# Strip attention on one core: 255 instead of 251 score tiles taken off ScalarE, in a new order, with GpSimd's constant add written another way

## The chip, the core and the metric

The kernel runs on one core of one Trainium2 chip. The metric is device time in microseconds (us), the median over several executions of the same program. Engines are called by the profile's names: PE is TensorE (matmuls), PEld its weight loads, DVE is VectorE, ACT is ScalarE, POOL is GpSimd, and SP is SyncE, which here only issues DMAs.

## The reference

An image of 224 x 224 pixels with 96 channels is projected to q, k and v. The first 48 channels attend inside horizontal strips 8 rows high, the last 48 inside vertical strips 8 columns wide; each strip has 1792 tokens, there are 28 strips of each kind. Both results are projected by `wo`.

```python
qkv = jnp.einsum('bhwc,cd->bhwd', x, wqkv)
q, k, v = qkv[..., :C], qkv[..., C:2*C], qkv[..., 2*C:]
scale = C2 ** (-0.5)                       # C = 96, C2 = 48, sw = 8, H = W = 224
qh, kh, vh = (t[..., :C2].reshape(B * nh, sw * W, C2) for t in (q, k, v))
ah = _softmax(jnp.einsum('bqc,bkc->bqk', qh, kh) * scale, axis=-1)
oh = jnp.einsum('bqk,bkc->bqc', ah, vh).reshape(B, H, W, C2)
# qv, kv, vv, av, ov: the same over vertical strips, channels C2 to C
o = pad(oh) + pad(ov)                      # side by side in the channels
return jnp.einsum('bhwc,cd->bhwd', o, wo)
```

The inputs are bf16: x of shape (1, 224, 224, 96), wqkv (96, 288), wo (96, 96).

## The kernel before

**Tiling.** Two strips are worked on together as one strip pair P, 28 in all: 0 to 13 horizontal, 14 to 27 vertical. Queries come in four chunks of 512, 512, 512 and 256 columns, keys in 14 blocks of 128. A score tile is one key block against one query chunk for both strips, 128 x 1024 values (for the last chunk two key blocks share one tile). PE makes the scores, something takes their exponential into a slot of `PT` (28 slots), and PE multiplies the slot by V and adds it up in one PSUM bank (the PV step).

**Who takes the exponential.** Mostly ACT, one ACTIVATE of 128 x 1024 for each tile (line 939, `emit_qk`). ACT's scores go to two fixed sets of two PSUM banks, in turn. The tiles listed in `KINDS`, one row for each P and one string for each chunk, are taken off ACT and get a polynomial in the bits of the result, of which there are two kinds in use:

- a **P tile**: DVE makes a scaled score q into `qb` (line 1082, two half tiles), POOL squares it (line 1110), adds a constant (line 1111) and squares again (line 1106); PE computes the scores a second time, and DVE adds them to the result as an integer (line 1087, two half tiles).
- an **R tile**: DVE makes q (line 1082) and a product with the scores (line 1084), two half tiles each, POOL squares (line 1106), PE computes the scores a second time, and DVE finishes (line 1087).

So a P tile is three POOL and four DVE instructions, an R tile one POOL and six DVE instructions. Some pairs of half tiles go through DVE as one instruction of 128 x 1024. Scores for DVE go to a ring of four PSUM banks, shared with PV sums and with the preparation of later strip pairs.

**Other work.** DVE also evicts the projections K, Q, V (lines 594, 603, 641), the PV sums (`OT`, line 958) and the output rows (`og`, line 709). A DMA transpose on SP turns `OT`; DVE takes reciprocals (line 1030) and POOL multiplies by them (line 1045, the norms, 54 in all). At the end POOL issues a few of the output DMAs.

**The order.** While the program is built, a planner walks the string list `ORDER`, one string for each P, a letter for each PE step: q is an ACT tile's scores, 1 and 3 the first and 2 and 4 the second scores of a P or R tile, v a PV step, k, g and f preparation and output steps. PE's instruction order is these strings, word for word. The planner keeps a clock for each engine from constants at the head of the file, and with it decides the order of DVE's and POOL's instructions (`dve_step`, `pool_step`), which slots and banks are used, and where SP's transfers stand. At run time each engine goes through its fixed list, and waits on semaphores of the engines (one count for each instruction) for what it reads or overwrites. POOL's instruction also waits for an earlier POOL instruction whose result it reads. When PE goes from scores (mode `A`, with f) to PV and preparation (mode `B`) or back, the planner adds a price, `SW_AB` or `SW_BA`.

The constants of the planner that matter here are its prices for POOL, in us: `D_SQ` for a product, `D_AF` for the constant add, `SEMP` for the time until a POOL result is seen; a norm's price is worked out in `dve_step` when its reciprocal is queued.

Of the kernel before, what the change touches and what calls it, by code (L numbers as in the profile page):

```python
# [30 lines left out]
    ["PR", "P", "PPRR", ""],
    ["RRPP", "RP", "PRRP", ""],
    ["RP", "RP", "PPPRR", ""],
    ["PRR", "P", "PPPRR", ""],
    ["PPRR", "P", "PRPRP", ""],
    ["PRR", "P", "PPRP", ""],
    ["PR", "RRP", "PPPRRP", ""],
    ["RR", "PP", "PPRRP", ""],
    ["PRP", "PPPR", "RP", ""],
    ["RP", "P", "RPPPRR", ""],  # L40
    ["RPR", "P", "PPPRPR", ""],
    ["RRP", "P", "PPRRP", ""],
    ["PR", "RPPPR", "PR", ""],
    ["PP", "RRPPR", "P", ""],
    ["PPPR", "RPP", "RRPP", ""],
    ["PR", "PPPRP", "P", ""],
    ["PPR", "R", "PPRP", ""],
    ["PPPRR", "PP", "R", ""],
    ["PPPP", "RR", "PRPP", ""],
    ["PPR", "R", "PPPP", ""],  # L50
    ["PPP", "RRRPR", "PP", ""],
    ["PPR", "PP", "RRPP", ""],
    ["PR", "PPP", "RRPP", ""],
    ["PP", "PP", "PRR", ""],
    ["PPP", "RRPR", "RPP", ""],
# [24 lines left out]
D_V2 = 0.6  # L80
# [4 lines left out]
    "vvq2vqv1qkvvqvvq2qvvqkvkq1qkvqvkvq1vqvkqkqkvvq2qvkvq1qkvqvvq1qvvvqkvqv4qvvq2qvvq1q1qvvkqvvvqv2qvq2qv2qvq2vqv1qvvq",
    "2vqvvvq2vqv3qvvqkkq1vqkvq1qkvvqkvq1vqvvvqv2qvvqkvvqkqk1qkqvvvqv1qvvqvvqv2qvvq1qvkq1qvvkq1qvvvkqvvq2qvvq2qvv1qvq2vqv2qvvvqv2qvq",
    "1vvq4qvvkqkkq1qvvkqvvvq1qvvvqkvq2vqvkvq1qvvq1qkvqvvqv2qvvq1qvkq2qvkqkvkq3qvvqvvqvvvq2qkvvq1vvq2qvv2qvvq2vqv1qvvqv1qvvq",
    "2vqv1qvvqk2qvkqkvq1qkvvqkvqv1qvkvqvvqv2qvvqv2qvvq1qvkq2qvkq1qkvqvvq1vvqvvqkvqvvqv2qvvq2vqv1qvvq2vqkvq2vqv3qvvvqk2qvvq1vvq",
    "2qvv1qvq2vqkvqkkvq1qkvqvkvqv1qvkqvvqv3qvvqv2qvvq1qvkq2qkvq1qkvqvvq1vvqvvqv2qvvqvvqvkq2vqv1qvkqv2qvvq2vvq2qkvvq2vqvvq1vq",
    "v2qvvqv1qkvvqvvqv1qvkqkvq1qkvvqkq2vqvkvq1qvvqk2qvvq1qvkq1qkvqvvq1vqvvvqv2qvvqkvqvvq2vqv1qkvqv2qvvq2vvq2qvv3qvvqv2qkvvq",  # L90
    "1qvv2qvvqkkqk1qvqkvvqvkvq2qvkvq1qvkq1qvkq1qkvqvvqv2qvkqvvq1qkvqvvq1vqvvqvv2qvvqvvqv2qkvvq1qvv1qvq2vvq2qvv2qvvq1vqvvq2vqv2q",
    "vvq1vqv1qvkvqvvq2qvvqkkvq1qkvqvkvq1vqvkqkqkvvq4qkvvq1qkqvvvq1vqvvvqv2qvvq1qvvq2qvvvq2vqv2qvvq2vqv1qvvq2vqkvkqvvq1vvq",
    "1qvv4qvvqk2qvkqkvq1qkvqvkvq1vqvvqvvq2vqvkvqv1qvvq1qvkq2qvkq1qkvqvvvq2qvvkqkvqv1qkvqvvvq2vqv2qvvq2vqv1qvvq2vvq1qvvq2vvqv2q",
    "vvq1vqv2qkvqkvq1qkvvqvkqv1qvvqvvvq1vqvkvqkqk2qvvq2qkvq1qkvvqvq1vvqkvq2qkvq2qvvq3vqvvq1vkqvvqv1qvvqv2qvvq2vvq2qvvq2vqvv2q",
    "vvq1vqvkq1vqkvq1qkvqvvkvq1qvvqvkvq2vqvkqkqkvvq1qkvvqvvq1vqvkqkvq1qkvqvv2qvvq2qvqvvq2vvq1qvv2qvvq2vqv2qvvq1vqvvq2vvq1qvv1q",
    "vq2vqv1qvvkqvvvq1vqvkqkvq1qkvqvvq2qvvkqv2qkqkkqkqk1qvvkqvvqv1qvvqvvqv1qvvqkvvq2qvkvqv2qvvq1vvq2qvv2qvq2vvq1qvv2qvvqv2q",
    "vvq1vqvkq2vqkvq1qkvqvvkvq1qvvvqvvq2vqvkvqkqk1qvvq1qvkqkkq1qkvqvvq1vqvvqvv2qvqvvq2vqvv2qvvq2qvv1qvq2vvq1qvv2qvqkvvq1vvq2q",
    "vv2qvqv1qkvqvvvq1vqvkqkvq1qkvvqkvq2vqvkqkvvq1qvvgqkqkvgqgkqkvqv2qvvq2vqv1qvvq2vqv1qvvvqvq1vqvvqvv1qvqv2qkq2qvvq3vqvvq2vvq",
    "2qvv2qvvqkkqkq1vqkvvqvvkq1qvgvqkgqkqkvq2vqv1qvkqkvq1vqgvvqvgq2vqkvqkgvq2vqv2qvvq1vqgvq2vqv1qvvqvvq1vqvvqvv1qvvqgvqgvq1vqvvq2vq",
    "v2qvvq2vqv1qvgvqvvq1vqvvqvv2qvqkvqkvkqkvvq1qvvkq3qkvvq2vqv2qvvq4vqgvq2vqvkq1vqv1qvvqgvqvvqkgqkkqgqgvq1vvq4qkvvq2qkvvq",  # L100
    "2qv1qvvvqv1qvvq2vqvkqk2qvvqgvkq1qkvvqkvq1vqvkqkvqgvq4vqgvq1vqvkqk2qvvqkvq1vqkvqkvgq2vqv2qvvq2vqvgq1vqv1qvvgqvvqv1qvvqvvgqv4qvvq",
    "v1qvvqv2qvvq1vq4qvvkqkq1kqvvkqvvkq2qvvqkvvq3vqvgq4vqgvq2vqv2qvvqkvq1vqv1qgvqvkq2vqv2qkvqkvq1vqkvq1vqvvvqv1qvvqvvkqv4qvvqv4qvvq",
    "v1qvvq2vqv1qvvqk1qvvqkvvqvkqkvqggvqkgqk2qvvvq2vqv3qvvqg2qvvqv1qvgqvkq2vqv1qgvqvkq4vqvgq1vqkkqkvqv1qvvkqvgqvvq1vqvgvqvvq1vqvvq2vq",
    "vvvq2vqv2qvvqkkqk1qvqkvvqvvq2vqvvq1vkqv1qvkqv2qvvqk4qvvqvgq2vqv1qgvqkvq1vqkgqv4qvkqv1qkvqvvqvvq1vqvkvqvvq4vqvvq2vvqv1qvvq",
    "v2qvvq1vqv2qvkqkkqvvkqggqkvqg1qvkqkgqkqkkqkvvq2vqv1qvvq1vqgvq2vqv2qvvqv1qkvvq2vqv2qgvqv1qgvqv2qgvqv1qvvqvvgqv1qvvqvvqv1qvvvqvvq",
    "vvqv2qvvq1vqvkq2kqvvq1qvvkqvvqkvvq2qvv1qkvq3vqvvq2vqv2qgvqgvgqkvqkq2vqkvq1vqkkqv2qgvqv2qvkqv1qvvqkvgq1qgvvqvvq2vqvvq2vvq",
    "1qvvvqv1qvvq2vqv4qvvqk1qvkqvvvq1qvvvqvvq2vqvvqkkvqv1qvvqkgq1vqkvq2vqvkq2vqv1qgvqvkq2vqv4qvvqk1qvvqvkqvvkqgvq1qkvvq2vqv2qvvq",
    "1vqv2qvvqgvq1vqv4qvvqk1qkvqvvqv1qvvqvvq2vqvgqkvqgvkqgvvqk1qvvq1vqkvq2vqkvq2vqv1qgvqvkq2vqv1qvvqg2qvvqkkqgvgqgvqkkvqv2qvvq2vq",
    "v1qvvq1vqv2qvvvq2qvv1qvvqkkq1qvkvqvvkqv1qvqvvvq4qvvvqkgqgkqvvq2vqkvq1vqv1qgvqkvq2vqv2qvkqvkq4vqkvq1vqv1qvvgqvvqv1qvvqvvqgvqv2qvvq",
    "kvvq1vqv2qvvq2vqv1qvgvqvvq1vqvvqvvq1vqvkqkvkqvvq2vqkvqvkgq1vqkvq2vqv1qgvqkvq2vqv2qvgqvkqvgqg1qvvqkkqgvkq2qvkvqv1qvvq2vqv2q",  # L110
    "vvq1vqvvvq2vqv1qvvq1vqvvqv1qvvqvvvq2vqvgqgvqgvq1vqvvq2vqv2qvvq2vqv1qvvfqv1qvfqv2qvfqvvfqvvfqv2qvvfqgvqgvq2vqv2qvvgqfvq4fqqvvvvvfffvvvfff",
# [106 lines left out]
def bass_standalone__window_attn_cswin__vision_kernel(  # L218
# [28 lines left out]
    with es:  # L247
# [844 lines left out]
        def mids_w(tl):  # L1092
            g, gk = gb[tl["gb"]], [("g", tl["gb"], 0), ("g", tl["gb"], 1), "pser"]
            l = g.bitcast(U16).rearrange("p (n t) -> p n t", t=2)[:, :, 0]
            y, yk = PT[tl["slot"]][:], pt_keys(tl["slot"])
# [2 lines left out]
            return [("pool", D_AF, lambda e: e.tensor_scalar(z, l, WK ** 0.5 * 2.0 ** -16, -WK ** 0.5 * t0, ALU.mult, ALU.add), gk, yk),
                    ("pool", D_SQ, lambda e: e.tensor_tensor(z, z, z, ALU.mult), yk + ["pser"], yk),
                    ("pool", D_AW, lambda e: e.tensor_tensor(g[:], g[:], z, ALU.add), gk + yk, gk[:2]),  # L1100
                    ("pool", D_AG, lambda e: e.tensor_scalar(y.bitcast(U16), g[:], c, 1.0, ALU.add, ALU.mult), gk, yk),
                    ("pool", D_AG, lambda e: e.tensor_scalar(PT[tl["slot2"]][:].bitcast(U16), g[:], c + 64.0, 1.0, ALU.add, ALU.mult), gk, pt_keys(tl["slot2"]))]

        def mids(tl):
            y, yk = PT[tl["slot"]][:].bitcast(FP16), pt_keys(tl["slot"])
            square = ("pool", D_SQ, lambda e: e.tensor_tensor(y, y, y, ALU.mult), yk + ["pser"], yk)  # L1106
# [3 lines left out]
            return [("pool", D_SQ, lambda e: e.tensor_tensor(y, q, q, ALU.mult), qk, yk),  # L1110
                    ("pool", D_AF, lambda e: e.tensor_scalar(y, y, -(QS * (RB + RA) / 2) ** 2, 1.0, ALU.add, ALU.mult), yk + ["pser"], yk),  # L1111
                    square]
# [521 lines left out]
```

## Time and profile before

| what | value |
|---|---|
| median of 3 runs | 1047.13 us (1046.86 to 1047.49) |
| the profiled execution's own time | 1047.03 us |
| its span, first to last instruction | 1045.2 us |
| granted TensorE clock, mean | 0.999 |
| busy: PE, DVE, ACT, POOL | 1024.8, 1027.6, 1034.9, 1001.9 us |
| ACT tiles, P tiles, R tiles | 1121, 155, 96 |

A row of a group reads: line, engine, operation, out<-in by the program's names, shape, xcount, then busy us and the mean ns of one, then the engine's idle time just before these instructions and what ended it. A row of the timeline reads: start in us, duration in us, engine, line, operation; equal neighbours are merged (x2), and a wait stands in brackets. Busy time is the union of the instructions' durations; where durations overlap, the step from start to start is shorter than a duration. Line numbers are those of the kernel before.

### The profile page before, as it was taken

The page shows a single profiled execution, that of the slowest core. Times are in us where ns is not written, and L with a number is a line of the kernel's source. Part 1 is how long each engine was busy: PE and PEld are TensorE (multiplying, and loading weights), DVE is VectorE, ACT ScalarE, POOL GpSimd, SP SyncE. Part 2 cuts the span into 40 slices and gives each one's busy share as a digit, 9 for nine tenths or more (in the row PEclk, how much of TensorE's full clock was granted, in tenths as well). Part 3 has the DMA queues.
Part 4 walks back from the last instruction along what each step waited for, and adds up shares of the span by engine and source line. Part 5 has one row for each costly group of instructions (what it writes and reads, how often), then busy time and mean ns, then how long its engine had stood idle before and what let it go on. Part 6 is the DMA issues. An engine that isn't in the chain of part 4 may idle for free.

```text
span 1045.2 us, 33013 instructions
## 1 busy us (share of the span) xinstructions
PE 1024.8 (98%) x13456; PEld 388.6 (37%) x13456; DVE 1027.6 (98%) x1905; ACT 1034.9 (99%) x1131; POOL 1001.9 (96%) x662
## 2 busy tenths in 40 slices
...
GB/s 175 166 181 126 131 24 140 119 52 125 147 93 71 130 108 81 28 59 59 15 91 114 60 93 103 101 58 94 95 49 104 105 100 44 104 102 49 71 79 60
DMA packets 414199, 96.84 MB, mean 93 GB/s; under 512 B 404928, under 2 KB 411296, under 8 KB 414048
## 3 DMA queue, kind: packets, MB, share of 16 engines
...
q0 software_dynamic: 128, 0.20, 0.1%
...
## 4 chain that ended last, share of the span: by engine, by line
PE 59%; DVE 24%; ACT 8%; issue 4%; POOL 4%; DMA 1%; POOLq 0%; ACTq 0%; SPq 0%; DVEq 0%
PE ps L788 23%; PE ps L761 20%; PE ps L774 10%; ACT PT L939 8%; DVE qb L1082 7%; DVE PT L1087 7%; DVE PT L1084 3%; PE ps L589 3%; DVE KT_sb L594 2%; PE ps L703 2%; POOL PT L1106 2%; PE ps L634 2%; DVE OT_sb L958 1%; DVE QT_sb L603 1%; POOL PT L1110 1%
## 5 line engine op out<-in xcount | busy, mean ns | idle before, releaser
L939 ACT ACTIVATE PT<-ps 128x1024 bf16<-128x1024 f32 x1121 | 1030.3, 1091 | 0.6 <-PE ps L761 0.2
L1106 POOL TENSOR_TENSOR PT<-PT 128x1024 f16<-128x1024 f16 x251 | 470.4, 1893 | 8.6 <-DVE PT L1084 1.0
L788 PE MATMUL ps<-PT,V_sb 128*49 128x512 bf16 (+1 forms) x3136 | 470.1, 362 | 0.3 <-DVE PT L1087 0.2
L761 PE MATMUL ps<-QT_sb,KT_sb 49*64 49x512 bf16 (+1 forms) x5292 | 456.4, 361 | 2.6 <-ACT PT L939 1.5
L1082 DVE TENSOR_SCALAR qb<-ps 128x512 f16<-128x512 int16 x490 | 329.8, 697 | 3.2 <-PE ps L761 0.3
L1087 DVE SCALAR_TENSOR_TENSOR PT<-ps,PT 128x512 uint16<-128x512 f32 (+1 forms) x479 | 323.0, 709 | 5.2 <-PE ps L774 0.9
L1110 POOL TENSOR_TENSOR PT<-qb 128x1024 f16<-128x1024 f16 x155 | 291.9, 1892 | 9.8 <-DVE qb L1082 6.5
L761 PEld LDWEIGHTS ps<-QT_sb,KT_sb 49*64 49x64 bf16 x5292 | 136.9, 104 | 264.0 <-ACT PT L939 240.3
L774 PE MATMUL ps<-QT_sb,KT_sb 54*64 54x512 bf16 (+1 forms) x2008 | 202.6, 394 | 11.7 <-DVE PT L1087 2.7
L788 PEld LDWEIGHTS ps<-PT,V_sb 128*49 128x49 bf16 x3136 | 133.2, 103 | 202.6 <-issue 169.8
L1111 POOL TENSOR_SCALAR PT<-PT 128x1024 f16<-128x1024 f16 x155 | 161.8, 1044 | 13.0
L1084 DVE SCALAR_TENSOR_TENSOR PT<-ps,qb 128x512 f16<-128x512 int16 (+1 forms) x190 | 128.0, 688 | 0.6
L774 PEld LDWEIGHTS ps<-QT_sb,KT_sb 54*64 54x64 bf16 (+1 forms) x2008 | 56.8, 103 | 101.0 <-DVE PT L1087 34.2
L958 DVE CAST OT_sb<-ps 113x512 bf16<-113x512 f32 x111 | 68.5, 617 | 0.1
L603 DVE CAST QT_sb<-ps 128x512 bf16<-128x512 f32 (+1 forms) x111 | 67.5, 615 | 0.1
L594 DVE TENSOR_SCALAR_CACHE_REDUCE KT_sb<-ps 128x512 bf16<-128x512 f32 x108 | 64.4, 616 | 0.0
L709 DVE CAST og<-ps 128x480 bf16<-128x480 f32 x84 | 50.8, 616 | 0.2
L641 DVE CAST V_sb<-ps 128x480 bf16<-128x480 f32 (+1 forms) x84 | 50.8, 617 | 0.1
L589 PE MATMUL ps<-xT_sb,wq_sb 97*64 97x512 bf16 x224 | 41.5, 368 | 0.0
L589 PE MATMUL ps<-xT_sb,w_sb 97*64 97x512 bf16 x224 | 39.8, 369 | 0.0
L634 PEld LDWEIGHTS ps<-w_sb,xT_sb 96*64 96x64 bf16 x1568 | 33.6, 112 | 16.3 <-issue 7.5
L634 PE MATMUL ps<-w_sb,xT_sb 96*64 96x48 bf16 x1568 | 39.3, 190 | 0.0
...
## 6 DMA issues: line engine op xcount, KB each, us to landing
...
```

What stands on the lines that cost most here:

```text
L589: ins = e.matmul(bk[64 * w:64 * w + 64, 0:qs], lhsT=lw, rhs=xT_sb[b][0:C + 1, w, q0:q0 + qs], start=True, stop=True)
L634: ins = e.matmul(bk[64 * h:64 * h + 64, j * C2:(j + 1) * C2], lhsT=xT_sb[b][0:C, w, t0:t0 + 64], rhs=w_sb[0:C, wblk(P, "v"), 0:C2], start= ...
L761: ins = e.matmul(bank(SETS[s] + w)[64 * kh:64 * kh + 64, i * t["qs"]:(i + 1) * t["qs"]], lhsT=KT_sb[b][64 * w:64 * w + CA, kt * 128 + 64 * ...
L774: ins = e.matmul(bank(bp[w])[64 * kh:64 * kh + 64, 0:512], lhsT=KT_sb[b][64 * w:64 * w + nr, kt * 128 + 64 * kh:kt * 128 + 64 * kh + 64], ...
L788: ins = e.matmul(bank(pb)[64 * w:64 * w + CA, 0:t["qs"]], lhsT=V2_sb[b][:, w, kt - NKT + NV2, :] if second else V_sb[b][:, w, kt, :], rhs= ...
L939: S.commit("act", 0.0, D_ACT, None, lambda e, s=s, slot=slot: e.activation(PT[slot][:], ps[:, 512 * SETS[s]:512 * SETS[s] + 1024], ACTF.Ex ...
L1082: fn, reads, writes = lambda e: e.tensor_scalar(q, l, m, a, ALU.mult, ALU.add), bk, qk
L1084: fn, reads, writes = lambda e: e.scalar_tensor_tensor(y.bitcast(FP16), l, -RA * 2.0 ** 16, q, ALU.add, ALU.mult), bk + qk, ptk
L1087: fn, reads, writes = lambda e: e.scalar_tensor_tensor(y.bitcast(U16), f, 128.0, y.bitcast(FP16), ALU.mult, ALU.add), bk + ptk, ptk
L1106: square = ("pool", D_SQ, lambda e: e.tensor_tensor(y, y, y, ALU.mult), yk + ["pser"], yk)
L1110: return [("pool", D_SQ, lambda e: e.tensor_tensor(y, q, q, ALU.mult), qk, yk), ("pool", D_AF, lambda e: e.tensor_scalar(y, y, -(QS * (RB ...
L1111: ("pool", D_AF, lambda e: e.tensor_scalar(y, y, -(QS * (RB + RA) / 2) ** 2, 1.0, ALU.add, ALU.mult), yk + ["pser"], yk),
```

## The change

Four things are edited; all else stays.

1. `KINDS`: 157 P and 98 R tiles instead of 155 and 96, 1117 ACT tiles instead of 1121, most rows different.
2. `ORDER`: all 28 strings are new.
3. The planner's prices for POOL: a product 1.852 instead of 1.9, the constant add 1.01 instead of 1.03, 0.125 more (`D_TS`) for a constant add that follows a product or a norm, 0.13 instead of 0.10 until a result is seen, a norm's fixed part 0.14 instead of 0.18. They steer the order of DVE's and POOL's instructions.
4. POOL's constant adds compute x times 1 plus c instead of x plus c times 1. Of the lines that have this, only line 1111 is used here: `KINDS` has no W and no Q tiles.

```diff
 KINDS = [
-    ["PR", "P", "PPP", ""],
-    ["RPR", "PP", "RRPRR", ""],
...
-    ["PP", "P", "PPRRPPP", ""],
+    ["PR", "P", "PPR", ""],
+    ["PPP", "R", "PRRP", ""],
...
+    ["PPR", "P", "PRRRPPP", ""],
 ]
-SEMD, SEMP, SELF, SEMX = 0.15, 0.10, 0.19, 0.05
+SEMD, SEMP, SELF, SEMX = 0.15, 0.13, 0.19, 0.05
-D_H, D_F, D_SQ, D_AF, D_M2 = 0.604, 1.137, 1.9, 1.03, 0.055
-D_AW, D_AG = 2.1, 1.03
+D_H, D_F, D_SQ, D_AF, D_M2 = 0.604, 1.137, 1.852, 1.01, 0.055
+D_AW, D_AG, D_TS = 2.088, 1.01, 0.125
-D_V2 = 0.6
+D_V2 = 0.65
 ORDER = [
-    "qqkkqkkq1qkkq3qkvvqvvqvkq1qkvvq2vvq1qvv2qvkqkvqvkkq1qvvvkqv1qkvq4vqvkq2vqv1qvvqvvqv1qvvvq1vqkqvvqvkq2vqv2qvkqv2qkvqkvqv1qvvkqv1q",
...
+    "qqkkqkkq3qkkq1qkvvqvqkvvq1qkvvq2vqv2qvvq1vqvkvqvkq1vqkkvqv1qkvqvkqkkqvvq1vqv2qvkqv1qvkqv2qvvqkvq2vqkvq2vqv1qkvvq1vqvvqvv2qvvqv2q",
...
-            return [("pool", D_SQ, lambda e: e.tensor_tensor(y, q, q, ALU.mult), qk, yk),
-                    ("pool", D_AF, lambda e: e.tensor_scalar(y, y, -(QS * (RB + RA) / 2) ** 2, 1.0, ALU.add, ALU.mult), yk + ["pser"], yk),
+            return [("T", D_SQ, lambda e: e.tensor_tensor(y, q, q, ALU.mult), qk, yk),
+                    ("S", D_AF, lambda e: e.tensor_scalar(y, y, 1.0, -(QS * (RB + RA) / 2) ** 2, ALU.mult, ALU.add), yk + ["pser"], yk),
                     square]
...
-        ..., dur=0.18 + 48 * n * 0.0016875))
+        ..., dur=0.14 + 48 * n * 0.0016875))
...
+                z["dur"] += D_TS if z["z"] < 0 and tm["pk"] == "T" else 0.0
+                tm["pk"] = "T" if z["z"] >= 0 else "S"
...
-            tm["pool"] = st + m[1]
-            tl["mid_t"] = st + m[1] + SEMP
-            S.commit("pool", 0.0, m[1], m[1] + SEMP, m[2], m[3], m[4])
+            d = m[1] + (D_TS if m[0] == "S" and tm["pk"] == "T" else 0.0)
+            tm["pk"] = m[0]
+            tm["pool"] = st + d
+            tl["mid_t"] = st + d + SEMP
+            S.commit("pool", 0.0, d, d + SEMP, m[2], m[3], m[4])
```

More of the change, by code (lines that the diff above doesn't have):

```diff
@@ L28 @@
 KINDS = [
-    ["PR", "P", "PPP", ""],
-    ["RPR", "PP", "RRPRR", ""],
[L31 to L55, printed above, removed]
-    ["PP", "P", "PPRRPPP", ""],
+    ["PR", "P", "PPR", ""],
+    ["PPP", "R", "PRRP", ""],
+    ["RRP", "RR", "PPRRPP", ""],
+    ["R", "R", "PRPPRRPP", ""],
+    ["PP", "PRPPR", "R", ""],
+    ["P", "PRRP", "PPRRP", ""],
+    ["RP", "R", "PPPRRPR", ""],
+    ["RP", "PP", "PPRR", ""],
+    ["PR", "PRP", "PPRR", ""],
+    ["PRRP", "PPP", "RR", ""],
+    ["PPR", "P", "RPPPRRP", ""],
+    ["R", "RPPPPR", "RP", ""],
+    ["PR", "PPPR", "PRRP", ""],
+    ["RPP", "PRPP", "RRP", ""],
+    ["R", "PPRPP", "RR", ""],
+    ["PP", "RRRPP", "RPP", ""],
+    ["PPPR", "PPRP", "P", ""],
+    ["P", "PRRPP", "RRP", ""],
+    ["PP", "PRPPPR", "R", ""],
+    ["PPR", "R", "PPP", ""],
+    ["PPPR", "PRPPR", "RP", ""],
+    ["PPP", "RPP", "RRPP", ""],
+    ["PP", "PPP", "RRP", ""],
+    ["RPP", "RPP", "RPP", ""],
+    ["PRP", "P", "PRP", ""],
+    ["RPPP", "RPRRP", "P", ""],
+    ["PP", "RPPP", "RP", ""],
+    ["PPR", "P", "PRRRPPP", ""],
 ]
@@ L79 @@
 D_G = 0.042
-D_V2 = 0.6
+D_V2 = 0.65
 ORDER = [
-    "qqkkqkkq1qkkq3qkvvqvvqvkq1qkvvq2vvq1qvv2qvkqkvqvkkq1qvvvkqv1qkvq4vqvkq2vqv1qvvqvvqv1qvvvq1vqkqvvqvkq2vqv2qvkqv2qkvqkvqv1qvvkqv1q",
[L85 to L111, printed above, removed]
@@ new lines @@
+    "1vqvvvqv2qvqvv1qvq2vvq3qvvkqkkq1qvvkqvvkq1qvvvqkvqv3qvvq2qvkq2qkvqv2qvvq2qvkqkvkqv1qvvq2vqv1qvvqvvvq2qvvvq2vqv1qvvqvvvq1vqv1q",
+    "kvqv2qvvvq2qvv1qvvqkkqk2qvvq1qkvqvvq1vqvvvqv2qvvqkvvq1qkkqkkq2qvvq1qkvvqkvqv3qvvqv2qvvq2vqvvq2vqv1qvvqvvvq1vqv2qkvvq1q",
+    "vvvq2vqv1qvq2vvq2qvvqkkkq1qvvvkqvvq1qvvvqkvq2vqvvkq1qvvq1qkvqvvvq1qvvqvvq2vqvkqkvqkvq4vvqvq1vvq2qvv1qvq2vvq2qvkvq2qkvvq",
+    "1vqv2qvvvq1qvv1qvvq2vqkqkvkq1qkvqvvq1vqvvvqv2qvvqkvvq2qkkqkkq1qvvq1qkvvqkvqv4qvvqv1qvvq2vqvvq2vqv1qvvqvvvq2vqv1qkvvq2vqvvq2vq",
@@ new lines @@
+    "v1qvq1vvq2qvvkqk1qkqvvkqvvvq1qvvvqkvq2vvqkvq1qvvqk2qvvq2qvkq1qkvqvvq1vqvvvqv2qvqvvvq2qvvkqv1qvkqv1qkvvq2qvv1qvq2vvqv2qvvq",
+    "2qvv1qvq2vqvkkq1qvvkqvqkvvq1vvqvqkvvq2vqkvq1qvkqv2qvvq1qvkqkkq1qkvqvvkqv3qvvq2qvvq2vqvv2qvvvq1qvvvqvvq1vvq2qvv2qvq4vqvvq",
+    "2vvq1qvv1qvq2kqvvkqkvq1qkvvqvq1vvqvvqv3qvvqvkq2qkkqkqk1qvvkqvvqv1qvvqvkqkvvq4qvvvvq2qvvvvq1qvv1qvq2vvq2qvv2qvq2vqv2q",
+    "vvvq1qvv3qvvqkkqk2qvvq1qkvqvkq1vqvvvqv4qvvq1qvkq2qvvqk2qvvq1qvkq1qkvqvvq2vvqkvqv1qvvq2vqv2qvvqv1qvkqv1qkvvq2vqv1qvvvqvq",
@@ new lines @@
+    "v2qvvvq2vqv1qvkqvkkq1qvvkqvvqv1qvvqvvkqv2qvvqkvvq2q4qkvvq1qvkq2qvkq1qkvqvvq1vqvkvqv1qvvq4qvvvq2vqv1qvkqv2qvvq1vqvvvqvvq",
+    "2kqvvq1vvq2qvv1qvq2kqvvqkvkq1qkvqvvq1vqvvvqv1qvqkvvq2qkkqkkq2qvvkqkvq1qkvqvvq2vqvvvq2vqv1qvvqv2qvvq1vvq2qvv2qvq1vqvvvq",
+    "v4qvvqv1qvq1vvq2qvvkqk1qkqvvkqvvvq1qvvvqkvqv2qvvkqkqkkqkvvq2qvvvq1vqv2qvvq2vkqvq1vvq2qkvvq1vvqvvqv1qvvqvvq2qvvq1qvqvvvqg1qvvq",
+    "1qvvq2vqvv2q2qvvqkkqgvqgvkq1qkvqvkvq1qvvkqkqkkqgvq2vqv1qvgqv2qvvqv1qvgvqkkqv2qgvqv2qgvqv1qkvvq2vqv1qvvqgvgqgq1qgvvvqv4q",
@@ new lines @@
+    "vvqv2qvvq1vqv2qvvvq1qvv2qvqv1qkvvqvvq1vqvkqkvq2qkvvvq2qkvvkq1qvkqv2qvvvq2vqkqkvkq1qvv4qvkqv1qkvvq4qvvgqv1qvgqvvqv4qvvq1qvvvq",
+    "gvqgvqvgq1vqv2qvvvq1qgvvq4vqvkq2kqvvq1qkvvqvkqv1qvvvqvvq1vqvkvq2qvvvq2vqvkqkq1vvq2qkvqkgqkvq1vqkvq1vqvvkqggqggq2qvvgq1qvvq",
+    "vvvq2vqv1qvq2vvq1qvv2qvvqv2qvvq1vqvkq2kqvvq1qkvqvkvvq1qvvvqvvkqv2qvqkkqv2qvvvq2qkvvq1qvv1qvkqkvq4vqkvq2vqv1qvvqvvkqv1qvvqvvq",
+    "v2qvvqgvq1vqv2qvvqv1qgvqv1qvvqkkqk2qvvqkvgqgvgqgvkqg2qvkqgvqkvq1qvvkq3qvgvq2vqv2qvvqv1qkvqkvq1vqvvqvv2qkqkvvq1vqv2qvvqgvgq1qgvqvvq",
@@ new lines @@
+    "2vqvvvq2vqv1qvvqv2qvvq2vqv1qvvqkkqk1qvvvkqvvq1qvvqvkvq3vqvvq2vqvkqkkq2qvvvq1qvv2qgvqv2qgvqv1qvkqvgq2vqvkqvgqk1qvvqkvgq",
+    "1qgvvqvv2qvvqvq2vvq1qvv2qvvqv2qvvq1vqv1qkvqvvvq1qvvvqvvq2vqvkqkvqkvvq2kqvvq1vvq1qvv2qvkqkqkgqv1qvgqv2qvkqkvq1vqv2qvvqgvkq",
+    "kvgq1qgvq2qvvq1vqv2qgvvq2vqv1qvvqv1qvvqvvvq2qvkvq1qvvqkvqvkvq1qvkvvq2qkvvkq2qvvkq2qvvvqkq1vqvvvqv2qvkqvkq1vqkvq1vqv2qvvq1qkvvq",
+    "vv2qvvqgqgvvq4vqgvq1vqv2qvvvq1qvv4qvvqk1qvvqkvqvvgqgqgvvkq2qvvq1vvq2qkvvvq2qvkvq1vvq2qkvvvq3qvkvq1vqvvqkqvvkq2qgvvqkgqgvq1qkvvkq",
@@ new lines @@
+    "v1qvvq4vqvgq4vqvgq1vvq2qvvvvq2qvgvvqkkqk1qvqkvvqkvvq2qvkvq1qvkqv1qvvqvvqv2qvvvq2vqv1qgvqv1qvgqv2qgvqv1qvkqkkqvkqv2qvvkq1qgvqvvvq2vq",
+    "vvq2qvv2qvvq1vqvvq1vqvvqvvqk1qvvqgvvqvkqgvkq1qvkqgvq2vvq2qvvvvq3qvvvgq2qkvvkq2qkvvq1qvv2qgvqv2qgvqv1qvvqkgqkqkvkq1qkvqvvq",
+    "v2qvvvq1vqv1qvvvq2qgvvvq2qvv3qvvqkkqk1qvvqvvvqgqkvvgq2qvkvq1vvq2qvvvkq2qvvvvq3qgvvq1vvq2qvvvkq2qvvv1qkqvvqvvvq2vqkqkvgqgvqkvq1vqv2qkvq",
+    "vvq2vvq1qvv2qvvq1vqvvqv1qvvvqvvq1vqvqvvgqvvq2qggqvvvq1vqv2qgvqv1qvvfqv2qvq1vqv2qvvvfqvfqvvffqvgqv4qgvqv2qgvvq2qv4qfvqfqfvvvvvffvfvvfff",
```

21 lines of the change are left out of this document (12 added, 9 removed).

## Prediction

> **What bounds the kernel now.** I read the page's totals first, then a window over the steady part, then GpSimd's groups, its timeline and its waits, and last VectorE and TensorE in the timeline.
>
> ```profile
> span 1045.2 us, 33013 instructions
> PE 1024.8 (98%) x13456; PEld 388.6 (37%) x13456; DVE 1027.6 (98%) x1905; ACT 1034.9 (99%) x1131; POOL 1001.9 (96%) x662
> L939 ACT ACTIVATE PT<-ps 128x1024 bf16<-128x1024 f32 x1121 | 1030.3, 1091 | 0.6 <-PE ps L761 0.2
> 10.00:1036.00 1026.00, 1012.12 (x13302) 380.91 (x13300) 1016.40 (x1857) 1025.49 (x1118) 992.27 (x635) 1.00 0.53 92
> ```
>
> The last row is the window from 10 to 1036 us; its columns are PE, PEld, DVE, ACT, POOL, granted clock, DMA. Four engines stand between 96 and 99%, so shares of busy time name no bound. ACT does one exponential (exp) per tile, 1121 of them in 1030.3 us: 0.919 us each, with 0.6 us of named idle. Taking tiles off ACT shortens the program only if POOL and DVE, which then get them, can still keep pace. POOL seems to have 4% left. Its rows say otherwise:
>
> ```profile
> L1106 POOL TENSOR_TENSOR PT<-PT 128x1024 f16<-128x1024 f16 x251 | 470.4, 1893 | 8.6 <-DVE PT L1084 1.0
> L1110 POOL TENSOR_TENSOR PT<-qb 128x1024 f16<-128x1024 f16 x155 | 291.9, 1892 | 9.8 <-DVE qb L1082 6.5 <-PE ps L761 0.3 <-PE ps L589 0.2
> L1111 POOL TENSOR_SCALAR PT<-PT 128x1024 f16<-128x1024 f16 x155 | 161.8, 1044 | 13.0
> L1045 POOL TENSOR_TENSOR ohn<-OT_tr,rn 128x672 bf16<-128x672 bf16 x28 | 36.7, 1314 | 0.7
> ```
>
> Call the two-input products T (L1106, L1110) and the constant add S (L1111). The 13.0 us of idle before S has no releaser: nobody is being waited for. The timeline (start, duration, instruction) shows what it is:
>
> ```profile
> 12.97 1.89 POOL L1110 TENSOR_TENSOR PT<-qb 128x1024 f16<-128x1024 f16 x1 [3.40 <-DVE qb L1082]
> ...
> 33.39 2.17 POOL L1111 TENSOR_SCALAR PT<-PT 128x1024 f16<-128x1024 f16 x2
> 35.64 5.59 POOL L1106 TENSOR_TENSOR PT<-PT 128x1024 f16<-128x1024 f16 x3
> 41.19 1.89 POOL L1110 TENSOR_TENSOR PT<-qb 128x1024 f16<-128x1024 f16 x1
> 43.04 1.89 POOL L1106 TENSOR_TENSOR PT<-PT 128x1024 f16<-128x1024 f16 x1
> 45.02 1.04 POOL L1111 TENSOR_SCALAR PT<-PT 128x1024 f16<-128x1024 f16 x1
> 46.15 1.89 POOL L1106 TENSOR_TENSOR PT<-PT 128x1024 f16<-128x1024 f16 x1
> ...
> 1034.48 1.89 POOL L1106 TENSOR_TENSOR PT<-PT 128x1024 f16<-128x1024 f16 x1
> 1036.34 0.74 POOL L336 DMA_DIRECT2D out_dram<-og  x1
> ```
>
> Read starts, not durations. A T followed by a T costs 41.19 to 43.04, 1.85 us, less than its 1.89. A T followed by an S costs 43.04 to 45.02, 1.98: entering S costs 0.13. An S costs 45.02 to 46.15, 1.13, and two of them 33.39 to 35.64, 2.25: 1.12 to 1.13 where its duration is 1.04. So the gaps round S are POOL's own price. What it really waits for is in the waits (total, times, longest):
>
> ```profile
> POOL PT L1110 <- DVE qb L1082: 6.5, 6, 3.4
> POOL PT L1106 <- DVE PT L1084: 1.0, 2, 0.5
> POOL stg L1045 <- DVE rn L1030: 0.4, 1, 0.4
> POOL stg L1045 <- ACT PT L939: 0.3, 1, 0.3
> POOL PT L1110 <- PE ps L761: 0.3, 1, 0.3
> ```
>
> Without the 3.4 us ahead of its first tile these are 5.1 us, in a stretch from 12.97 to 1036.34. POOL, at "96%", is full to about half a per cent, and is the tightest engine here.
>
> **The change, part by part.** *Tiles.* Counting letters in the lists, P goes from 155 to 157 and R from 96 to 98. ACT loses 4 x 0.919 = 3.7 us. Its lead-in and tail keep their steps (the last chunk still drains through a dozen products and output rows), so I put nothing there. If POOL and DVE follow, the profile's span falls by 3.7.
>
> *POOL, new work.* A P tile issues T, S, T; an R tile one T. The extra 2 P + 2 R are 6 T and 2 S: 6 x 1.85 + 2 x (1.12 + 0.13) = 13.6 us at today's prices, against 5.1 us of waits. The norms (L1045) keep their number.
>
> *POOL, the new form of S.* No instruction of this trace multiplies by one and then adds, so the price must be bounded. One end is no saving, 1.12: the same elements through the same operation, in another order of its two steps. A loss on S is not excluded by any row; its far end is a T, 1.85, but nothing is read or written beside what S does now, so I give that end no weight. The nearest one-input rows are the copies:
>
> ```profile
> L396 POOL COPY wq_sb<-wst 96x96 bf16<-96x96 bf16 x4 | 1.0, 262 | 0.2
> L404 POOL COPY w_sb<-wst 96x192 bf16<-96x192 bf16 x1 | 0.3, 339 | 0.7 <-DMA wst<-in_wqkv_dram 0.7
> ```
>
> 96 more elements cost 77 ns, so a copy of 1024 would last 262 + 928 x 0.80 = 1.01 us, by estimate, where S lasts 1.04. Kept between gaps as S is now, that saves 0.04. If S were also followed as closely as a T is (0.04 before its end, where S is followed 0.08 after it), its step would be 1.04 - 0.04 = 1.00, a saving of 0.12. The diff puts 1.01 into its plan. A plan's constant is a claim, but its neighbours can be tested: it plans T at 1.852, entry into S at 0.125, and a norm of 14 blocks at 0.14 + 48 x 14 x 0.0016875 = 1.274; the trace has 1.85, 0.13, and 1.314 less the 0.04 overlap. Three are right as start-to-start steps, and the fourth is off by 0.11 for the old form alone. I take 1.01, with the ends 1.00 and 1.12. Then the 155 old S give back 155 x 0.11 = 17.1 us, the new work is 13.6 - 2 x 0.11 = 13.4, and POOL ends 3.7 us lighter: just what ACT loses. The entries into S, at 0.13 each and at most one for each S, could move this by a few us either way.
>
> A rule speaks against this. The Trainium skill, GPSIMD Engine Reference, section 3.1, says that an elementwise body of up to two operations is bound by its ports at 1.03 cycles an element, so that swapping two operations would change nothing in the loop. By it S stays at 1.12 and the sum is the first rival's.
>
> *The price from which it pays.* POOL is over by 13.6 - 5.1 = 8.5 us if S keeps its price; 8.5 / 157 = 0.054 us saved on each S makes it even, (8.5 + 3.7) / 157 = 0.078 makes room for all of ACT's gain. The copies' 0.04 is too little, 0.11 is enough.
>
> *DVE.* A P tile is four half-tile operations, an R tile six: 20 more.
>
> ```profile
> L1082 DVE TENSOR_SCALAR qb<-ps 128x512 f16<-128x512 int16 x478 | 315.2, 684 | 2.9 <-PE ps L761 0.3 <-PE ps L774 0.2
> L1087 DVE SCALAR_TENSOR_TENSOR PT<-ps,PT 128x512 uint16<-128x512 f32 x456 | 294.9, 683 | 4.3 <-PE ps L774 0.7 <-POOL PT L1106 0.2
> 509.15 0.68 DVE L1084 SCALAR_TENSOR_TENSOR PT<-ps,qb 128x512 f16<-128x512 int16 x1
> 509.75 0.68 DVE L1087 SCALAR_TENSOR_TENSOR PT<-ps,PT 128x512 uint16<-128x512 f32 x1
> 510.35 0.68 DVE L958 CAST OT_sb<-ps 113x512 bf16<-113x512 f32 x1
> ```
>
> Back to back they step by 0.60, so 20 cost 12.0 us. From 10 to 1036 us DVE is visibly idle for 1026.0 - 1016.4 = 9.6 us, and more is hidden: when no successor is ready, the 0.08 of tail beyond the step counts as busy. I take it that the hidden part covers the rest, at nothing; if it does not, the second rival's price applies. The cover is thin.
>
> *PE.* The string of steps changes between the QK group (q, 1 to 4, f) and the PV and preparation group (v, k, g) 2010 times before and 1874 after.
>
> ```profile
> 700.32 0.40 PE L788 MATMUL ps<-PT,V_sb 128*49 128x512 bf16 x2
> 700.65 0.41 PE L774 MATMUL ps<-QT_sb,KT_sb 54*64 54x512 bf16 x4
> 700.89 0.39 PE L761 MATMUL ps<-QT_sb,KT_sb 49*64 49x256 bf16 x8
> 701.21 0.62 PE L788 MATMUL ps<-PT,V_sb 128*49 128x512 bf16 x4
> ```
>
> A step inside a group takes 0.24 (700.65 to 700.89), one that changes group 0.32 to 0.33: 0.09 each, 136 x 0.09 = 12 us less. 8 more score steps, less 4 q, add about 4 x 0.24 = 1 us. PE was not the last to end (see ACT's 0.6 us of idle), so I take nothing for it; it is a reserve in which PE absorbs waits for DVE.
>
> *Queues.* No semaphore is added, and SP's transfers keep their number; each is issued where the new order puts it, behind a norm that POOL may take up to one T (1.85 us) later, with tens of us until its block is used.
>
> *Sum.* The profiled execution took 1047.03 us (its span and 1.8 around it), the median is 1047.13. 1047.13 - 3.7 = 1043.4.
>
> **The rivals.** *A: the rewriting buys nothing; POOL becomes the bound.* S stays at 1.12 and POOL's stretch grows by 8.5 us; products come late, the second score step and the PV steps behind them hold PE, and ACT stands: 1047.1 + 8.5 = 1055.6. With the copies' 0.04 it is 8.5 - 6.3 = +2.2, 1049.3. It decides below 0.054 saved on S. For it: two steps are two steps in either order, and S already lies close to a copy. Against: the gaps round S, which a T lacks, show that there is more than the loop to save.
>
> *B: DVE becomes the bound.* 12.0 us of new work against 9.6 of visible idle: +2.4, 1049.5, if nothing is hidden; with 6.1 us hidden ACT's whole gain is kept. The place is a score step on PE, which waits for a pair of PSUM banks that DVE still has to read, with the next q queued behind it. For it: DVE's idle already comes in pieces under a microsecond. Against: 9.6 counts tails as work.
>
> *C: more than the tiles.* ACT's exponentials step by 0.919 on the average, but where nothing disturbs them by less:
>
> ```profile
> 499.58 8.36 ACT L939 ACTIVATE PT<-ps 128x1024 bf16<-128x1024 f32 x9
> ```
>
> With 1.09 for the last, eight steps take 7.27: 0.909. All 1117 at that would be 11 us less. With 12 us of relief on PE and true POOL prices in the plan, a third is possible: 1043.4 - 3.7 = 1039.7.
>
> **How the numbers follow.** A measurement of this kernel can tell about 0.2%, 2.1 us, from no change: faster is below 1045.0, slower above 1049.2. The forecast has 0.56 (its own range is 1041 to 1045.3), C 0.09 (1037 to 1041), B 0.13 (1045 to 1050), A 0.22 (1049 to 1056). Faster: C and 0.53 of the forecast, 0.62. Same: 0.03 of the forecast and 0.07 of B, 0.10. Slower: A and the rest of B, 0.28. The range reaches from the middle of C, 1039.5, to the middle of A, 1052, and leaves out about 0.05 below and 0.12 above.
>
> **What would show it.** L939 x1117 with a mean step near 0.919; L1106 x255, L1110 x157 and L1111 x157 with S followed 1.01 us after its start and T unchanged at 1.85; DVE 12 us busier with no new wait of half a microsecond on it; PE with fewer "issue" gaps. A step of S at 1.08 or more, and a POOL without any wait, would prove A; a POOL with more waits for DVE and PE score steps waiting longer for DVE would prove B. If S costs 1.01 and the time still doesn't fall, the prediction's step from POOL's room to ACT's gain is what failed.

## The result and the profile after

The changed kernel takes 1060.9 us (median of 5 runs, 1059.21 to 1068.77) against 1047.13: a ratio of 1.0141, 95% interval 1.0107 to 1.0175, slower. Forecast was 1043.4, with 1039.5 to 1052 as the range. Run again beside the experiments it took 1057.76 us (1055.7 to 1059.84) where the kernel before took 1048.03: 1.0093 [1.0078, 1.0109]. Two executions far from all others (1145.56 us of the kernel before, 1886.38 of a run of it with a short add) are left out; apart from them the kernel before varies by 0.2%, the changed one by up to 1%, for a reason that its profile shows. The page after, from its execution of 1061.78 us:

```profile
span 1059.7 us, 33034 instructions
PE 1031.2 (97%) x13472; PEld 388.6 (37%) x13472; DVE 1034.4 (98%) x1926; ACT 1035.7 (98%) x1127; POOL 1015.3 (96%) x670
PEclk9999999999999999998999999999999999999997
L939 ACT ACTIVATE PT<-ps 128x1024 bf16<-128x1024 f32 x1117 | 1031.0, 1073 | 12.3 <-PE ps L761 11.3
L1106 POOL TENSOR_TENSOR PT<-PT 128x1024 f16<-128x1024 f16 x255 | 478.3, 1894 | 9.4 <-DVE PT L1084 2.0
L1110 POOL TENSOR_TENSOR PT<-qb 128x1024 f16<-128x1024 f16 x157 | 296.2, 1895 | 7.8 <-DVE qb L1082 4.9
L1111 POOL TENSOR_SCALAR PT<-PT 128x1024 f16<-128x1024 f16 x157 | 164.4, 1047 | 13.2
```

The constant add S did not get cheaper: a mean of 1047 ns where it was 1044, and 13.2 us of gap before it. POOL's timeline gives the step:

```profile
29.51 1.89 POOL L1106 TENSOR_TENSOR PT<-PT 128x1024 f16<-128x1024 f16 x1
31.49 1.05 POOL L1111 TENSOR_SCALAR PT<-PT 128x1024 f16<-128x1024 f16 x1
32.62 3.75 POOL L1106 TENSOR_TENSOR PT<-PT 128x1024 f16<-128x1024 f16 x2
```

Entering S takes 1.98, S itself 31.49 to 32.62, 1.13, as before. POOL has no named wait on DVE from its first tile, at 12.7 us, to 477 us: it is full. The new element is ACT's 12.3 us of idle, where there were 0.6, nearly all of it behind PE's score step, and one slice of lower granted clock in mid-run. Where that time went is seen at 470 us. First POOL, then DVE, then PE, each in the order of its start:

```profile
466.60 3.75 POOL L1106 TENSOR_TENSOR PT<-PT 128x1024 f16<-128x1024 f16 x2
470.30 1.90 POOL L1110 TENSOR_TENSOR PT<-qb 128x1024 f16<-128x1024 f16 x1
468.29 0.65 DVE L641 CAST V_sb<-ps 128x480 bf16<-128x480 f32 x1
470.45 1.29 DVE L1087 SCALAR_TENSOR_TENSOR PT<-ps,PT 128x512 uint16<-128x512 f32 x2 [1.50 <-POOL PT L1106]
469.63 0.41 PE L761 MATMUL ps<-QT_sb,KT_sb 49*64 49x512 bf16 x4
471.79 0.46 PE L774 MATMUL ps<-QT_sb,KT_sb 54*64 54x512 bf16 x4 [1.75 <-DVE PT L1087]
472.03 0.65 PE L761 MATMUL ps<-QT_sb,KT_sb 49*64 49x512 bf16 x4
```

DVE stands 1.50 us for a POOL square, and behind DVE PE stands 1.75 us in front of a score step, with the next ACT tile's scores queued behind. After that gap the same four matmuls of line 761 last 0.65 us instead of 0.41. The windows (PE, PEld, DVE, ACT, POOL, granted clock) show why, and that it is slow to heal:

```profile
470.00:475.00 5.00, 3.25 (x38) 0.99 (x34) 4.26 (x7) 2.93 (x4) 4.83 (x5) 0.70 0.03 4
475.00:480.00 5.00, 5.00 (x32) 1.22 (x34) 2.60 (x5) 2.99 (x4) 3.65 (x3) 0.50 0.49 68
480.00:485.00 5.00, 5.00 (x34) 1.05 (x30) 3.29 (x5) 3.42 (x4) 4.58 (x3) 0.50 0.00 0
```

At a granted clock of 0.50 PE is the bound, and 3 or 4 exponentials touch a window of 5 us there, where 7 and 6 touch the two windows from 440 to 450 us. There are two such places, one at 450 to 490 us and one at 900 to 960, and the tail, where the clock is at 0.50 for the last 11 us (in the kernel before for the last 2.5).

### The profile page after: what moved, and what is told of

It is laid out like the page before. It is cut to its first block, busy times and chain, and to the rows that moved or that the text cites. A ratio compares the mean times of both kernels' runs of the same rounds, so it can differ in the third digit from the quotient of the medians.

```text
span 1059.7 us, 33034 instructions
## 1 busy us (share of the span) xinstructions
PE 1031.2 (97%) x13472; PEld 388.6 (37%) x13472; DVE 1034.4 (98%) x1926; ACT 1035.7 (98%) x1127; POOL 1015.3 (96%) x670
## 4 chain that ended last, share of the span: by engine, by line
PE 45%; DVE 32%; POOL 10%; issue 6%; ACT 5%; DMA 1%; SPq 0%; DVEq 0%; POOLq 0%; ACTq 0%
PE ps L788 17%; PE ps L761 15%; DVE qb L1082 10%; DVE PT L1087 10%; PE ps L774 7%; ACT PT L939 5%; POOL PT L1106 5%; DVE PT L1084 4%; POOL PT L1110 3%; DVE KT_sb L594 2%; PE ps L589 2%; DVE QT_sb L603 2%; POOL PT L1111 2%; DVE V_sb L641 2%; DVE OT_sb L958 2%
## 5 line engine op out<-in xcount | busy, mean ns | idle before, releaser
L939 ACT ACTIVATE PT<-ps 128x1024 bf16<-128x1024 f32 x1117 | 1031.0, 1073 | 12.3 <-PE ps L761 11.3
L1106 POOL TENSOR_TENSOR PT<-PT 128x1024 f16<-128x1024 f16 x255 | 478.3, 1894 | 9.4 <-DVE PT L1084 2.0
L788 PE MATMUL ps<-PT,V_sb 128*49 128x512 bf16 (+1 forms) x3136 | 459.7, 365 | 0.3 <-DVE KT_sb L594 0.2
L1087 DVE SCALAR_TENSOR_TENSOR PT<-ps,PT 128x512 uint16<-128x512 f32 (+1 forms) x488 | 328.1, 705 | 9.8 <-PE ps L774 3.2
L1082 DVE TENSOR_SCALAR qb<-ps 128x512 f16<-128x512 int16 (+1 forms) x496 | 333.4, 699 | 3.6 <-PE ps L774 2.1
L1110 POOL TENSOR_TENSOR PT<-qb 128x1024 f16<-128x1024 f16 x157 | 296.2, 1895 | 7.8 <-DVE qb L1082 4.9
L774 PE MATMUL ps<-QT_sb,KT_sb 54*64 54x512 bf16 (+1 forms) x2040 | 207.7, 397 | 16.8 <-DVE PT L1087 7.8
L1111 POOL TENSOR_SCALAR PT<-PT 128x1024 f16<-128x1024 f16 x157 | 164.4, 1047 | 13.2
L1084 DVE SCALAR_TENSOR_TENSOR PT<-ps,qb 128x512 f16<-128x512 int16 x196 | 129.2, 681 | 0.2
```

Of the source, the lines that this page charges most:

```text
L774: ins = e.matmul(bank(bp[w])[64 * kh:64 * kh + 64, 0:512], lhsT=KT_sb[b][64 * w:64 * w + nr, kt * 128 + 64 * kh:kt * 128 + 64 * kh + 64], ...
L788: ins = e.matmul(bank(pb)[64 * w:64 * w + CA, 0:t["qs"]], lhsT=V2_sb[b][:, w, kt - NKT + NV2, :] if second else V_sb[b][:, w, kt, :], rhs= ...
L939: S.commit("act", 0.0, D_ACT, None, lambda e, s=s, slot=slot: e.activation(PT[slot][:], ps[:, 512 * SETS[s]:512 * SETS[s] + 1024], ACTF.Ex ...
L1082: fn, reads, writes = lambda e: e.tensor_scalar(q, l, m, a, ALU.mult, ALU.add), bk, qk
L1084: fn, reads, writes = lambda e: e.scalar_tensor_tensor(y.bitcast(FP16), l, -RA * 2.0 ** 16, q, ALU.add, ALU.mult), bk + qk, ptk
L1087: fn, reads, writes = lambda e: e.scalar_tensor_tensor(y.bitcast(U16), f, 128.0, y.bitcast(FP16), ALU.mult, ALU.add), bk + ptk, ptk
```

## The experiments

Theory 1 is rival A of the prediction: the new form buys nothing, POOL is over its room, and late POOL results stop PE. Against it stood B (DVE gave out) and a third, that the new order is at fault whatever POOL's load. Each run is set against the kernel before on the same chip; a short add or a short DVE operation stands for a price that the chip doesn't offer, and leaves some columns with a wrong value.

**The form alone, on the kernel before.**

```diff
-tensor_scalar(y, y, -(QS * (RB + RA) / 2) ** 2, 1.0, ALU.add, ALU.mult)
+tensor_scalar(y, y, 1.0, -(QS * (RB + RA) / 2) ** 2, ALU.mult, ALU.add)
```

> The kernel before with line 1111 alone rewritten as times one, plus constant; tiles, order and prices stay. Theory 1 (the form buys nothing, POOL's load is what failed): a constant add still steps by 1.12 to 1.13 us, and the time is 1047.1 within 1 us. Theory 2 (the form does save 0.1 us an add, and something else, DVE or the order, cost the time): the step falls to about 1.01, POOL gains 17 us of room, and the time falls below 1047 by up to a few us.

1047.61 against 1048.4 us: 0.9994 [0.9984, 1.0003]. The step is that of the old form:

```profile
44.85 1.04 POOL L1111 TENSOR_SCALAR PT<-PT 128x1024 f16<-128x1024 f16 x1
45.98 1.89 POOL L1106 TENSOR_TENSOR PT<-PT 128x1024 f16<-128x1024 f16 x1
```

1.13 us. The order of the two steps makes no difference, as theory 1 says.

**The changed kernel with the old form** (the edit above, backwards).

> The changed kernel with line 1111 in the old form (plus constant, times one); all else as changed. Theory 1 (form buys nothing): the same time as the changed kernel, 1059 to 1062, and the add's step is 1.12 to 1.13. Theory 2 (the form saves, other parts cost more): slower than the changed kernel by up to 17 us, 1070 or more.

1057.55 us (1054.41 to 1058.84): 1.0082 [1.0065, 1.0099], against 1.0093 [1.0078, 1.0109] for the changed kernel when it was run again. The form is worth nothing here either; the time lies below the 1059 to 1062 expected, as that of the changed kernel itself does when it is run again.

> The changed kernel itself, on the chip and in the rounds of the others of this call, so that they can be set against it. Theory 1 and its rivals alike: 1055 to 1062 where the kernel before takes 1047 to 1048.5.

1057.76 us, as said above. In its profile the same POOL wait at 470 us did not bring the clock down; the second place, at 950 us, did.

**The add at the price that the plan gave it.**

```diff
-tensor_scalar(y, y, 1.0, c, ALU.mult, ALU.add)
+tensor_scalar(y[:, 0:884], y[:, 0:884], 1.0, c, ALU.mult, ALU.add)
```

Here c stands for the constant.

> The changed kernel with the constant add on 884 of its 1024 columns, which leaves 140 columns without their constant, so that its step should be near the 1.01 us of the plan. PE, DVE and ACT keep their instructions word for word. Theory 1 (POOL's price alone sank the change): the long waits of PE and the stretches at half clock in mid-run go, and the time is near the forecast, 1042 to 1045. Rival (DVE, with 20 more half-tile operations, is what gave out): it stays above 1050, with waits for DVE that do not come from POOL.

1046.81 against 1048.4 us: 0.9984 [0.9974, 0.9993]. All other engines had their instructions word for word, and a loss of 9.7 us (run again) or 13.8 (first) became a gain of 1.6; the 1042 to 1045 expected were not reached. The same two POOL squares, the same DVE work and the step of S in this run:

```profile
31.14 0.93 POOL L1111 TENSOR_SCALAR PT<-PT 128x884 f16<-128x884 f16 x1
32.15 3.75 POOL L1106 TENSOR_TENSOR PT<-PT 128x1024 f16<-128x1024 f16 x2
462.77 3.74 POOL L1106 TENSOR_TENSOR PT<-PT 128x1024 f16<-128x1024 f16 x2
466.78 0.65 DVE L641 CAST V_sb<-ps 128x480 bf16<-128x480 f32 x1
467.38 1.29 DVE L1087 SCALAR_TENSOR_TENSOR PT<-ps,PT 128x512 uint16<-128x512 f32 x2
```

S steps by 1.01. The squares start at 462.77 where the changed kernel had them at 466.60: there POOL ran 3.8 us late in the changed kernel, while DVE ran only 1.5 late (468.29 against 466.78). In the short run the second square ends at 466.51, 0.87 us ahead of the DVE operation that reads it; 3.83 less 1.51 less 0.87 is the 1.5 us that DVE stood in the changed kernel. In the window from 450 to 500 us ACT's count is 56 here, 53 in the changed kernel run again and 46 in its first profile (after, again, short add):

```profile
450.00:500.00 50.00, 46.39 (x514) 15.25 (x516) 41.98 (x77) 42.75 (x46) 45.98 (x29) 0.86 0.17 33
```
```profile
450.00:500.00 50.00, 46.49 (x574) 16.58 (x568) 47.35 (x90) 48.02 (x53) 48.77 (x31) 1.00 0.20 41
```
```profile
450.00:500.00 50.00, 48.56 (x594) 17.26 (x590) 49.75 (x94) 49.85 (x56) 48.33 (x31) 1.00 0.21 41
```

And from 900 to 960 us (after, again):

```profile
900.00:960.00 60.00, 57.17 (x750) 22.13 (x750) 56.64 (x106) 56.79 (x62) 58.69 (x38) 0.97 0.45 90
```
```profile
900.00:960.00 60.00, 56.85 (x730) 21.07 (x726) 55.02 (x105) 55.12 (x60) 58.59 (x38) 0.94 0.43 87
```

At the second place PE also stands in front of an output step (line 703) for a transpose on SP, which stands behind a norm on POOL. In the changed kernel's timeline and waits:

```profile
946.34 1.48 POOL L1045 TENSOR_TENSOR stg<-OT_tr,rn 128x768 bf16<-128x768 bf16 x1
947.85 1.94 SPq L477 DMA_TRANSPOSE oc_all<-stg  x1
953.08 0.45 PE L703 MATMUL ps<-wo,oc_all 96*64 96x96 bf16 x10 [1.26 <-DMA oc_all<-stg]
PEld ps L703 <- DMA oc_all<-stg: 1.6, 1, 1.6
```

The run with the short add has no such wait. A mean clock of 0.86 over 50 us is some 14 us at half clock, 0.97 and 0.94 over 60 us are 4 and 7. The short run has the same list of exponentials, so the two can be compared one by one: those of the changed kernel start 0.4 us later at 450 us, 8.7 later at 506 and 12.1 later at 948 (times of the short run), and the span ends 15.4 later, with some 3 us of the difference in the tail. In the changed kernel run again these are 0.7, 3.2, 8.6 and 9.2.

So in the first window POOL's lateness alone costs 3 tiles, and the half clock that may or may not follow another 7. This is why the changed kernel's times scatter: they go with the mean granted clock of the execution, from 1055.7 us at 0.996 to 1068.77 at 0.983. But 1.6 us is not the 3.7 of the forecast.

**A price in between** (954 columns instead of 884).

> The changed kernel with the constant add on 954 of 1024 columns, which leaves 70 columns without their constant: a step of about 1.07 us, 0.058 saved on each of 157. By the prediction's sum POOL is even with the kernel before at 0.054 saved. Theory 1 (time follows POOL's overload in proportion): about the kernel before, within 2 us of it, no half clock in mid-run. Rival (a few stalls with their half clock come all or nothing): still 5 us or more slower than before.

1046.99 against 1048.39 us: 0.9991 [0.9982, 1.0001]. S steps by 1.07 (the median of all is 1.074, and 1.125 in the changed kernel run again), 0.05 less than at full width, about the 0.054 that the prediction gave as even, and the time is even or a little better. Not in proportion, though: half of the saving brought nearly all of the time. POOL was without pause, and its named waits on DVE after the first tile shrank to 0.8 us:

```profile
POOL PT L1110 <- DVE qb L1082: 3.7, 2, 3.4
POOL PT L1106 <- DVE PT L1084: 0.5, 1, 0.5
```

The norm that starts at 946.34 us in the changed kernel and at 932.35 with the short add starts at 934.97 here, 2.6 us later than with the short add, and no wait follows from it; the profiled execution has half clock only from 1037 us, in the tail. So the plan tolerates a POOL that is late by some 2.5 us; by 3.8 us (at 470 us) it stalls. No run has a saving between nothing and 0.05.

**The short add on the kernel before.**

> The kernel before with the constant add on 884 of 1024 columns, which leaves 140 columns without their constant; its step should be 1.01 us as in the changed kernel with the short add, so POOL gets 155 x 0.115 = 18 us of room and nothing else changes. Theory 1 (POOL is full in the kernel before but not what sets its end, ACT does): 0 to 2 us faster than before. Rival (POOL sets the end already before the change): faster by 5 us or more.

1047.55 against 1048.03 us: 0.9995 [0.9985, 1.0005]. With 18 us of POOL work gone nothing moved: POOL was full in the kernel before, but did not set its end, and the columns with a wrong value do not by themselves change the time. Set against this, the four tiles fewer on ACT, with the new order, are worth 1.1 us (0.9995 to 0.9984), not 3.7.

**DVE's part.**

```diff
+if h != 2:
+    f, y = f[:, 0:480], y[:, 0:480]      # the half tiles of line 1087
```

> The changed kernel with the short constant add (884 of 1024 columns) and with DVE's last operation of a tile, line 1087, on 480 of its 512 columns where it is a half tile; the columns left out keep a wrong value. DVE gets about 450 x 0.033 = 15 us of room. With the short add alone the kernel was 1.6 us faster than before where 3.7 was forecast. Theory B (DVE's thin cover took the other 2.1 us): another 2 us or more faster, at least 3.5 us below before. Rival (the new order itself costs ACT those 2 us, or ACT's own pace does): within 0.8 us of the short add alone, that is 0.8 to 2.4 us below before.

> The changed kernel with the full constant add and only DVE's line 1087 shortened to 480 of 512 columns. Theory 1 (POOL is over its room and DVE has little part in it): 2 us or less faster than the changed kernel in this call, still 6 us or more slower than before. Theory B (DVE is the one that gave out): most of the loss goes, within 2 us of the kernel before.

> The control for the short add with short DVE: the kernel before with both (884 of 1024 columns of the add, 480 of 512 of line 1087 where it is a half tile; those columns keep a wrong value). With both, the changed kernel was 3.3 us faster than before, with the short add alone 1.6. Theory B (the 20 more DVE operations took those 2 us, and the kernel before has DVE room enough): 0 to 1 us faster than before. Rival (any kernel here gains from a shorter DVE operation): 1.5 us or more faster than before.

Changed kernel with both: 1044.77 against 1048.03 us, 0.9968 [0.9956, 0.998], 3.3 us faster, between the two expectations. Changed kernel with only DVE short: 1058.35 us, 1.0096 [1.0077, 1.0115], the same as the changed kernel, so DVE's thin cover is not the cause of the loss. The control, the kernel before with both: 1045.91 against 1048.39 us, 0.9975 [0.9966, 0.9985]. I had expected the control to stay put; it gained as much as the changed kernel did. About 14 us of DVE room (the half tiles of line 1087 are busy for 287.5 us instead of 301.5) buy some 2 us in either kernel (0.9984 to 0.9968 and 0.9995 to 0.9975), about 0.13 us for each us: in these runs DVE acts less as a bound that one runs into than as a soft price. If work added costs what work removed gave, the 12.0 us of new DVE work took about 1.6 of ACT's 3.7, by estimate, and 2.1 should be left where 1.1 was measured, a difference that the intervals of about 1 us each do not resolve.

**The true price in the plan.**

```diff
-D_H, D_F, D_SQ, D_AF, D_M2 = 0.604, 1.137, 1.852, 1.01, 0.055
+D_H, D_F, D_SQ, D_AF, D_M2 = 0.604, 1.137, 1.852, 1.125, 0.055
```

> The changed kernel planned with 1.125 instead of 1.01 us for the constant add: the same tiles, PE's order word for word the same, but DVE's and POOL's orders and the PSUM banks worked out with the true price. Theory 1a (POOL's load against its room is the cause): still slower than before, 1050 to 1060, since 13.6 us of POOL work are still there. Theory 1b (not the load but a plan that had POOL's results in a wrong order was the cause): 1043 to 1047.

1078.85 us, 1.0289 [1.0262, 1.0316]: far beyond what either version of the theory expected. PE's order is the same to the letter, POOL has the same instructions at the same prices, yet it is worse by some 20 us than with the wrong price. Now PE's weight loads and POOL wait for DVE, in these two rows for 17.6 and 16.4 us where the changed kernel has 10.4 and 4.9:

```profile
PEld ps L774 <- DVE PT L1084: 17.6, 40, 1.8
POOL PT L1110 <- DVE qb L1082: 16.4, 14, 3.3
```

In this profile the clock is at 0.50 for 34 us in mid-run, against 17 and 7 in the two profiles of the changed kernel, so part of the 20 us is again half clock.

**Four P tiles made R**, and **the old tiles and order under the new prices.**

```diff
-    ["R", "R", "PRPPRRPP", ""],
+    ["R", "R", "RRPPRRPP", ""],
...
-    ["PPP", "RPP", "RRPP", ""],
+    ["RPP", "RPP", "RRPP", ""],
```

> The changed kernel with four of its P tiles (one each in strip pairs 2, 8, 14 and 20) made R tiles: POOL has 4 x 3.1 = 12.4 us less to do, DVE 4 x 1.2 = 4.8 us more, the reference's result, PE's order word for word the same; DVE's and POOL's orders are worked out anew. Theory 1 (POOL's overload of 8.5 us is the cause): the loss goes, 1046 to 1051. Theory 2 (any new DVE and POOL order under an unmoved PE order breaks the fit): slower than the changed kernel or equal to it, 1056 or more.

> The changed kernel's prices and form of the add with the tiles and the order of the kernel before: PE's order is the kernel before's, POOL's, DVE's and SP's orders are worked out anew. Theory 1 (load decides; the load is that of before): within 1.5 us of the kernel before. Theory 2 (an order is searched for its prices, and prices changed without a new search break it, as in the run planned with 1.125): 4 us or more slower than before.

The four R tiles gave 1068.78 us, 1.0207 [1.0181, 1.0233]: with 12 us less POOL work, some 10 us slower than the changed kernel, against the theory that the load alone decides, and with only 3.4 us at half clock before the tail. The old lists under the new prices gave 1049.67 against 1048.39 us, 1.0013 [1.0003, 1.0023]: a small loss, within the 1.5 us of the theory that the load decides. The bad two have more of DVE's and POOL's order moved under a fixed PE order: compared by line number with the kernel whose PE order they share, some 30 of DVE's 1926 instructions and 110 to 120 of POOL's 670 stand elsewhere in either, against 8 and 15 in this one. That this is the cause is not shown; slots and banks move with it. In the four-R run PE's weight loads and POOL wait for DVE's product of line 1084 (10.4 and 2.0 us in the changed kernel):

```profile
PEld ps L774 <- DVE PT L1084: 26.7, 47, 1.5
POOL PT L1106 <- DVE PT L1084: 11.6, 10, 4.5
```

So these order strings seem to go with the engine orders that they came with; a lighter POOL alone did not help when those moved. I have not isolated which single placement costs what; that stays open, and so does whether a search with the true price would find a use for 255 tiles. Of the kernels that do all the work, none beats the kernel before.

## Why the prediction was wrong

**The step that failed is the price of S.** It was put at 1.01, with 1.00 and 1.12 as the ends; both the changed kernel and the form alone measure 1.13, so the 17.1 us that were to pay for the new work never came; with the step brought to 1.01 by fewer columns, the loss is gone. I took the diff's constant because its three neighbours agreed with the trace to a few nanoseconds. Agreement of the neighbours vouches for how those were measured, not for one that no row showed. The rows that were there, the copies, put a one-input pass of this length at 1.01 long where S lasted 1.04, and said how little there was to save; the row nearest to the unknown should have had the most weight. The Trainium skill's rule that I cited against the change (GPSIMD Engine Reference, section 3.1, two operations cost no more than one in the loop) is borne out as to the swap: the form changed nothing, 1.13 before and after.

**Rival A's sum was nearly right.** 8.5 us over its room gave 1055.6; the two comparisons gave 1057.8 and 1060.9, beyond its own 1049 to 1056. Its break-even, 0.054 saved on each S, agrees with the run at 0.05, which is even; that it isn't lower is not shown. It had a chance of 0.22, and the range stopped in the middle of it.

**What A lacked is how POOL's lateness turns into time.** I had it as a stretch of POOL that gets longer, so that its sum came near is in part luck. In fact ACT kept pace for 450 us while POOL fell behind, then the program lost most of its time in two places, where PE stood for more than a microsecond, POOL could catch up, and PE then, in some executions, ran at half clock for 3 to 14 us. That is also why POOL still shows waits for DVE after 477 us, where the prediction had named a POOL without any wait as a sign of A. The term that was missing is the clock: in one window it cost about twice as much as the wait itself.

**ACT's gain was over-sized even without POOL.** 4 x 0.919 = 3.7 was to arrive whole; with POOL's price granted, 1.1 arrived against the same edit on the kernel before, with intervals of about 1 us. Where the rest went is not shown. The term put at nothing, DVE's cover, would by the soft price above take 1.6 of it (rival B was sized as a threshold); what the new order itself costs was not tested.

**A norm's cover was not there.** The prediction put a norm's lateness at nothing, with tens of us until its block is used. Near 950 us a norm ended at 947.82, and PE, which stood 1.26 us for the transpose behind it, began its output step at 953.08.

**Right:** POOL is full where the page shows 96%; T, the norms and the entry into S kept their steps.
